# Second layer: the mixed rows of eight tiles turned by VectorE and DRAM in place of TensorE, the last SoLU rows too, and the decay table by four transposes

## The chip, the cores and the metric

One Trainium2 chip (trn2), one of its cores. The metric is the time of one execution on the device in microseconds, the median of three runs. Five engines work side by side, each through its own instructions in order: TensorE (PE in the rows; PEld is its weight load), VectorE (DVE), ScalarE (ACT), GpSimd (POOL) and SyncE (SP). SP computes nothing here; it issues most of the DMAs, in order, and waits in that order too.

## The reference

Three stages, each feeding the next: a retention layer, a top-2 mixture of eight experts, and a dense layer with SoLU and a row norm.

```python
# 1: batch 2, heads 8, seq 768, head_dim 64
state = gamma * state + k_t (outer) v_t;  y_t = scale * q_t @ state
# 2: x is 1536 x 512; w1 512 x 1024, w2 1024 x 512 for each of 8 experts
out[mask] += top2_w[mask, k, None] * (np.maximum(x[mask] @ w1[e], 0.0) @ w2[e])
# 3: w_in 512 x 1024, w_out 1024 x 512
h = x @ w_in
e = np.exp(h - np.max(h, axis=-1, keepdims=True))
solu = h * e / (np.sum(e, axis=-1, keepdims=True) + 1e-09)
ln = (solu - mean) / np.sqrt(var + 1e-06) * g_ln
return ln @ w_out
```

## The kernel before

The 1536 rows are 12 tiles of 128, numbered 0 to 11. The order of work is written out by hand, and each engine gets its instructions in that order. Products are made in two parts: an operand x becomes `hi` (x rounded to the narrower format fp32r, on ScalarE) and `lo` = x - hi (on VectorE), and a product is hi*hi + hi*lo + lo*hi, three passes.

**The start.** `scores(0)` multiplies keys and queries of tile 0 on TensorE, VectorE masks the result (`pm`). `dec_t(0)` (L291) makes a table of decays, one row per column of a head: eight products of a broadcast column of `dec` with the identity, copied to SBUF by ScalarE. `kv(0)` and `y_out(0)` follow on TensorE. They are the first of the retention layer's products; the expert layer comes next, and needs all of them.

**The second layer** (the reference's third stage) is the loop at L1226. Tile i passes through these steps, and iteration i works on several tiles at once:

- `gather` (L815): GpSimd fetches its rows from the experts' results, two gathers of 128 rows.
- `mix(i+4)` (L826): ScalarE and VectorE weigh and add them: 128 tokens x 512.
- `x2_t(i+3)` (L836): TensorE turns them with four transposes into a bank of PSUM; ScalarE copies `x2h` (L850) and VectorE subtracts `x2l` (L851).
- `h_in(i+2, 0)` and `h_in(i+2, 1)` (L854): the product with w_in, 12 passes of 512 columns each, into PSUM bank `d`. `x2_t(i+3)` stands between the two.
- `solu_max(i+2)` and `solu(i+2)` (L901, L906): maximum of the rows (VectorE, L871), exponential (ScalarE, L879), product and norm (VectorE, L880 to L885), which gives `z`.
- `z_turn(i+2)` (L932): VectorE turns `z` in blocks of 32x32 into `zs` (L935), SP writes it to DRAM in four DMAs (`zd`, L938) and loads it back turned (`zc`, L940). That load waits until the four writes have landed.
- `z_parts(i)` (L943): `zh` on ScalarE, `zl` on VectorE.
- `out_mm(i)` (L954): 24 passes with w_out, and in the next iteration `store_out` (L963).

Tiles 0 and 11 do not use `z_turn`: `z_t` (L911) turns them with eight transposes of TensorE. `z_t(11)` stands between `out_mm(9)` and `out_mm(10)`. `out_mm(11)` is made in two column halves, each with a store of its own.

Of the kernel before, what the change touches and what calls it, by code (L numbers as in the profile page):

```python
# [8 lines left out]
F32 = mybir.dt.float32  # L9
F32R = mybir.dt.float32r  # L10
# [5 lines left out]
AF = mybir.ActivationFunctionType  # L16
# [28 lines left out]
def retnet_moe_solu(ctx, tc, qT, kT, k, v, w_gate, w_noise, noise, w1, w2, w_in, w_out, g_ln,  # L45
                    decay, out, dbg=None):
    nc = tc.nc
    B, NC, _, H, D = v.shape
    HP = H // 2
    S = NC * 128  # L50
    NT = B * NC
    E = w1.shape[0]
    DM = H * D
    KD = DM // 128
    FF = w1.shape[2]
    KF = FF // 128
# [7 lines left out]
    dram = ctx.enter_context(tc.tile_pool(name="dram", bufs=1, space=DRAM))  # L64
# [84 lines left out]
    raw_t, unit_t, turn_of = {}, {}, {}  # L149
# [78 lines left out]
    wk = att.enter_context(tc.tile_pool(name="wk", bufs=2))  # L228
# [22 lines left out]
    dec = const.tile([128, 2, NC, H], F32, name="dec")  # L251
# [27 lines left out]
    ident = unit[0][:, G2:G2 + 128]  # L279
# [11 lines left out]
    def dec_t(c):  # L291
        if c >= NC:
            return
        decT[c] = wk.tile([128, HP, 128], F32, tag="decT" if c else "decT0", name="decT", bufs=2 if c else 1)
        if c:
            for hp in range(HP):
                nc.scalar.activation(decT[c][:, hp], decT[0][:, hp], AF.Copy, scale=step[:, c, hp:hp + 1])
            return
        p = bank("c3", (128, HP, 128))
        for h in range(H):  # L300
            r = slice(h % 2 * 64, h % 2 * 64 + 64)
            nc.tensor.matmul(p[r, h // 2, :], dec[:, 1, c, h:h + 1].to_broadcast([128, D]), ident, start=True, stop=True,
                             skip_group_check=True)
        nc.scalar.activation(decT[c], p, AF.Copy)

    def dec_steps():
# [35 lines left out]
    part = const.tile([128, 3], F32, name="part")  # L342
# [54 lines left out]
    for b in range(B):  # L397
        for r in range(2):
            t = wk.tile([128, HP, 128], F32, name=f"S{b}{r}", bufs=1)
# [411 lines left out]
    Y, X2, X2T, PH, ST, Z, RS, ZT = {}, {}, {}, {}, {}, {}, {}, {}  # L811
# [14 lines left out]
    def mix(i):  # L826
        if i >= NT:
            return
        y0, y1 = Y.pop(i)
        t = fr.tile([128, DM], F32, tag="t", name="t")  # L830
        w = top_w[:, i] if i else pick[:, 0]
        nc.scalar.activation(t, y0, AF.Copy, scale=w[:, 0:1])
        nc.vector.scalar_tensor_tensor(t, y1, w[:, 1:2], t, op0=OP.mult, op1=OP.add)
        X2[i] = t

    def x2_t(i):  # L836
        if i >= NT:
            return
        t = X2.pop(i)
        p = bank("a")  # L840
        y = None if i else last_y.pop()
        for d in range(KD):
            c = slice(d * 128, (d + 1) * 128)
            nc.tensor.transpose(p[:, c], t[:, c], ident)  # L844
            if y:
                nc.tensor.matmul(p[:, c], y[:, c], spread.rearrange("p a i -> p (a i)"), start=False, stop=True,
                                 skip_group_check=True)
        hi = fr.tile([128, KD * 128], F32R, tag="x2h", name="x2h")
        lo = fr.tile([128, KD * 128], F32R, tag="x2l", name="x2l")
        nc.scalar.activation(hi, p, AF.Copy)  # L850
        nc.vector.tensor_sub(lo, p, hi)  # L851
        X2T[i] = (hi, lo)

    def h_in(i, s):  # L854
        if i >= NT:
            return
        if s == 0:
            PH[i] = bank(f"d{i % 2}", (128, 2, 512))
        hi, lo = X2T[i]
        n = 0  # L860
        for d in range(KD):
            c = slice(d * 128, (d + 1) * 128)
            f = slice(s * 512, s * 512 + 512)
            wh, wl = unit_t[8 * E + d]
            for x, w in ((hi, wh), (hi, wl), (lo, wh)):
                nc.tensor.matmul(PH[i][:, s, :], x[:, c], w[:, 0, f], start=(n == 0), stop=(n == 3 * KD - 1))  # L866
                n += 1

    def row_max(pool, ph):
        t = pool.tile([128, 16], F32, tag="st", name="st", bufs=3)  # L870
        nc.vector.reduce_max(t[:, 0:1], ph, axis=AX.X)  # L871
        nc.vector.tensor_scalar_mul(t[:, 0:1], t[:, 0:1], -1.0)
        return t
# [27 lines left out]
    def solu_max(i):  # L901
        if i >= NT:
            return
        ST[i] = row_max(m2, PH[i].rearrange("p a f -> p (a f)"))

    def solu(i):  # L906
        if i >= NT:
            return
        Z[i], RS[i] = solu_rows(m2, PH.pop(i).rearrange("p a f -> p (a f)"), ST.pop(i))

    def z_t(i, between=lambda: None):  # L911
        hi = m2.tile([128, KF * 128], F32R, tag="zh", name="zh")
        lo = m2.tile([128, KF * 128], F32R, tag="zl", name="zl")
        z = Z.pop(i)
        ps = []
        for s in range(2):
            p = bank("a")
            for d in range(4):
                f = 4 * s + d
                nc.tensor.transpose(p[:, d * 128:(d + 1) * 128], z[:, f * 128:(f + 1) * 128], ident)  # L920
            c = slice(s * 512, s * 512 + 512)
            nc.scalar.activation(hi[:, c], p, AF.Copy)
            ps.append((p, c))
        for p, c in ps:
# [7 lines left out]
    def z_turn(i):  # L932

        t = m2.tile([128, 4, 256], F32, tag="zs", name="zs")
        nc.vector.transpose(t.rearrange("p g c -> p (g c)"), Z.pop(i).rearrange("p (k g c) -> p g k c", g=4, c=32))  # L935
        d = dram.tile([4, 32, 4, 256], F32, tag="zd", name="zd", bufs=3)
        for a in range(4):
            nc.sync.dma_start(d[:, :, a].rearrange("g i c -> i g c"), t[32 * a:32 * a + 32])  # L938
        t = m2.tile([128, 4, KF, 32], F32, tag="zc", name="zc")
        nc.sync.dma_start(t, d.rearrange("g i a (k j) -> (g i) a k j", j=32))  # L940
        ZD[i] = t

    def z_parts(i):  # L943
        hi = m2.tile([128, KF, 4, 32], F32R, tag="zh", name="zh")
        lo = m2.tile([128, KF, 4, 32], F32R, tag="zl", name="zl")
        t = ZD.pop(i).rearrange("p a k j -> p k a j")
        for k in (slice(0, KF // 2), slice(KF // 2, KF)) if i == 1 else (slice(0, KF),):
            nc.scalar.activation(hi[:, k], t[:, k], AF.Copy)
        ZT[i] = tuple(x.rearrange("p k a j -> p (k a j)") for x in (hi, lo))
        return lambda: nc.vector.tensor_sub(lo, t, hi)  # L950

    OUT = {}

    def out_mm(i, c=slice(0, DM)):  # L954
        hi, lo = ZT[i]
        p = bank("b")[:, c]
        terms = [(z, f, n) for z, ns in ((hi, (0, 1)), (lo, (0,))) for f in range(KF) for n in ns]
        for m, (z, f, n) in enumerate(terms):
            nc.tensor.matmul(p, z[:, f * 128:(f + 1) * 128], unit_t[8 * E + 4 + f // 2][n][:, f % 2, c],  # L959
                             start=(m == 0), stop=(m == len(terms) - 1))  # L960
        OUT[i] = p

    def store_out(i, c=slice(0, DM)):  # L963
        o = m2.tile([128, DM], F32, tag="o", name="o", bufs=3)
        nc.scalar.activation(o[:, c], OUT.pop(i), AF.Copy, scale=RS[i])
        (nc.scalar if c.stop == DM and c.start else nc.sync).dma_start(out[row0(i):row0(i) + 128, c], o[:, c])


    ep = ex_ctx.enter_context(tc.tile_pool(name="ep", bufs=1, reuse_waits="tile"))
# [253 lines left out]
    feed(n_units, n_units)  # L1223
    h_in(1, 1)

    for i in range(NT):  # L1226
        gather(i + 5)
        low = None
        if i == 0:
            z_t(0, lambda: solu_max(1))  # L1230
            solu(1)
            z_turn(1)
            RS[0] = RS[0]()
        else:
            if i < NT - 1:
                low = z_parts(i)
            store_out(i - 1)
        if i + 1 < NT:
            RS[i + 1] = RS[i + 1]()
        h_in(i + 2, 0)  # L1240
        if low:
            low()
        x2_t(i + 3)
        mix(i + 4)
        h_in(i + 2, 1)
        solu_max(i + 2)
        solu(i + 2)
        if i + 2 < NT - 1:
            z_turn(i + 2)
        if i == NT - 2:  # L1250
            z_t(i + 1)
        if i < NT - 1:
            out_mm(i)
        else:
            for c in (slice(0, DM // 2), slice(DM // 2, DM)):
                out_mm(i, c)
                store_out(i, c)
# [135 lines left out]
```

## Time and profile before

| | |
|---|---|
| median of 3 runs | 514.53 us (514.43 to 514.70) |
| the profiled execution | 515.7 us, of which the span from the first to the last instruction is 513.9 us |
| mean granted clock of TensorE | 0.998 |
| busy: TensorE, VectorE, ScalarE, GpSimd | 506.6, 364.6, 233.2, 106.3 us |
| second layer | from 369.1 us (first product of `h_in`) to 510.0 us |

The profile's times are microseconds from the first instruction, of one execution; its span is compared with other spans, its own time with the runs. A busy time counts an instruction from its start to its end, and TensorE's instructions overlap, so the distance from start to start says more than the length of one.

### The profile page before, as it was taken

The numbers are of one execution on the slowest core, as the hardware profiler recorded it, in microseconds if no ns is written. First come the engines' busy times: TensorE is split into PE (matmuls) and PEld (weight loads), VectorE is DVE, ScalarE is ACT, GpSimd is POOL, SyncE is SP. The second block draws the span as 40 slices with busy tenths as digits, with TensorE's granted clock in tenths as the row PEclk, the third lists the DMA queues.
The fourth block names the chain that finished last, engine by engine and source line by source line (L and its number), as shares of the span: only waits on it lengthen the run. The fifth ranks groups of instructions, "written<-read, shape, count | busy, mean of one in ns | idle before, by whom it ended". The sixth has DMA issues, their size and how long they took to land.

```text
span 513.9 us, 8633 instructions
## 1 busy us (share of the span) xinstructions
PE 506.6 (99%) x3068; PEld 463.9 (90%) x3068; DVE 364.6 (71%) x731; ACT 233.2 (45%) x440; POOL 106.3 (21%) x209
## 2 busy tenths in 40 slices
PE   9999999999999999999999999999999999999996
PEld 8898898989999999999999999998878888888885
DVE  4668778756876886877778778799277767666650
ACT  2578734443353443344435443545354644444431
POOL 4124100513002104004003000002244336311120
PEclk9999999999999999999999999999999999999999
DMA  8989531797978988979899968568553565643341
GB/s 259 347 319 368 208 103 42 243 348 266 328 225 230 294 248 203 352 199 283 296 239 324 288 200 237 198 172 222 160 190 106 166 184 149 206 134 103 102 123 47
DMA packets 71857, 111.92 MB, mean 218 GB/s; under 512 B 9760, under 2 KB 37152, under 8 KB 71808
## 3 DMA queue, kind: packets, MB, share of 16 engines
q1 hardware_dynamic: 65952, 96.54, 61.5%
q0 software_dynamic: 4368, 14.29, 8.9%
q10 hardware_dynamic: 1488, 0.48, 0.4%
q8 instruction: 26, 0.43, 0.4%
q14 instruction: 23, 0.19, 0.1%
HBM read 83.50 MB, written 27.79 MB: 217 GB/s over the span
## 4 chain that ended last, share of the span: by engine, by line
PE 90%; issue 5%; DMA 2%; DVE 2%; POOL 1%; ACT 0%; POOLq 0%; ACTq 0%; DVEq 0%
PE c L1077 23%; PE b L959 13%; PE b L729 12%; PE a L729 12%; PE d L866 11%; PE c L1200 3%; PE xr L480 3%; PE s L430 3%; PE c L447 2%; PE c L458 2%; PE c L443 2%; DMA xr<-xd,rows_r 2%; PE a L844 1%; PE c L269 1%; DVE wl L197 0%
## 5 line engine op out<-in xcount | busy, mean ns | idle before, releaser
L201 DVE TENSOR_TENSOR wl<-wr,wh 128x1024 fp32r<-128x1024 f32 x64 | 76.7, 1219 | 13.5 <-ACT wh L200 13.5
L1077 PE MATMUL c<-hh,wh 128*128 128x448 f32 (+5 forms) x224 | 79.1, 353 | 0.0
L1077 PE MATMUL c<-hl,wh 128*128 128x448 f32 (+5 forms) x224 | 78.9, 352 | 0.0
L1077 PE MATMUL c<-hh,wl 128*128 128x448 f32 (+5 forms) x224 | 78.8, 352 | 0.0
L200 ACT ACTIVATE wh<-wr 128x1024 fp32r<-128x1024 f32 x68 | 69.4, 1049 | 8.5 <-DMA wr<-in_moe_w_dram 8.5
L729 PE MATMUL b<-xh,wh 128*128 128x192 f32 (+8 forms) x144 | 47.2, 335 | 0.2 <-ACT xh L644 0.2
L729 PE MATMUL b<-xh,wl 128*128 128x192 f32 (+8 forms) x144 | 46.7, 332 | 0.0
L1077 PEld LDWEIGHTS c<-hh,wl 128*128 128x128 f32 x224 | 42.2, 188 | 1.3
L1077 PEld LDWEIGHTS c<-hh,wh 128*128 128x128 f32 x224 | 42.1, 188 | 1.3
L1077 PEld LDWEIGHTS c<-hl,wh 128*128 128x128 f32 x224 | 42.1, 188 | 1.3
L729 PE MATMUL a<-xh,wh 128*128 128x256 f32 (+7 forms) x128 | 43.1, 341 | 0.0
L729 PE MATMUL a<-xh,wl 128*128 128x256 f32 (+7 forms) x128 | 42.9, 339 | 0.0
L866 PE MATMUL d<-wh,x2h 128*128 128x512 f32 x96 | 38.8, 404 | 0.0
L959 PE MATMUL b<-wh,zh 128*128 128x512 f32 (+1 forms) x104 | 38.4, 375 | 0.0
L959 PE MATMUL b<-wl,zh 128*128 128x512 f32 (+1 forms) x104 | 38.4, 375 | 0.0
L866 PE MATMUL d<-wl,x2h 128*128 128x512 f32 x96 | 37.9, 395 | 0.0
L866 PE MATMUL d<-wh,x2l 128*128 128x512 f32 x96 | 37.8, 394 | 0.0
L1115 POOL COPY pace<-hh 1x1 f32<-1x1 f32 x20 | 9.7, 485 | 135.4 <-ACT hh L733 135.4
L733 ACT ACTIVATE hh<-b 128x192 fp32r<-128x192 f32 (+8 forms) x36 | 17.1, 475 | 43.6 <-PE b L729 40.9
L733 ACT ACTIVATE hh<-a 128x256 fp32r<-128x256 f32 (+7 forms) x32 | 15.9, 496 | 45.8 <-PE a L729 45.8
L1040 ACT ACTIVATE xh<-xt 128x428 fp32r<-128x428 f32 (+5 forms) x24 | 13.0, 540 | 45.1 <-DVE xt L1038 45.1
L1004 POOL DMA_INDIRECT xr<-xd,rows_r x27 | 28.1, 1040 | 25.4 <-DVE rows_r L677 15.9
(258 smaller groups left out, 1091.5 us busy)
## 6 DMA issues: line engine op xcount, KB each, us to landing
wr<-in_moe_w_dram SPq DMA_DIRECT2D x64, 512.0 KB
zd<-zs SPq DMA_DIRECT2D x40, 128.0 KB
zc<-zd SPq DMA_DIRECT2D x10, 512.0 KB
xs<-xr SPq DMA_DIRECT2D x18, 256.0 KB
raw<-in_moe_w_in_dram SPq DMA_DIRECT2D x8, 512.0 KB
raw<-in_moe_w_out_dram SPq DMA_DIRECT2D x8, 512.0 KB
xq<-xs SPq DMA_DIRECT2D x16, 208.0 KB
yg<-yr SPq DMA_DIRECT2D x16, 208.0 KB
```

What stands on the lines that cost most here:

```text
L200: nc.scalar.activation(hi, t, AF.Copy)
L201: (nc.gpsimd if u < LEAD else nc.vector).tensor_sub(lo, t, hi)
L430: nc.tensor.matmul(p[:, s, hp, :], KT[i][r, hp, :], QT[i][r, hp, :], start=True, stop=True)
L480: nc.tensor.matmul(t[:, d // 2, at:at + 128 + G2], XT[i][:, d, :], unit[d // 2][:, G2 - G2 * (d % 2):][:, :128 + G2], start=(d % 2 == 0), ...
L729: nc.tensor.matmul(p, w[:, 0, f * 128:(f + 1) * 128], x[:, d, c], start=(n == 0), stop=(n == len(terms) - 1))
L733: nc.scalar.activation(hh[:, f, c], p, AF.Relu)
L866: nc.tensor.matmul(PH[i][:, s, :], x[:, c], w[:, 0, f], start=(n == 0), stop=(n == 3 * KD - 1))
L959: nc.tensor.matmul(p, z[:, f * 128:(f + 1) * 128], unit_t[8 * E + 4 + f // 2][n][:, f % 2, c], start=(m == 0), stop=(m == len(terms) - 1))
L1004: nc.gpsimd.indirect_dma_start(out=t[b], out_offset=None, in_=xd[:], in_offset=bass.IndirectOffsetOnAxis(ap=rows_r[:, e - 1, b:b + 1], axi ...
L1040: nc.scalar.activation(hi, t, AF.Copy)
L1077: nc.tensor.matmul(py[d][:, :CAPS[e]], c, h[:, f, :CAPS[e]], start=(f == 0 and n == 0), stop=(f == KF - 1 and n == 2))
L1200: nc.tensor.matmul(py, h[:, f, c], w[:, f % 2], start=(f == 0 and n == 0), stop=(f == KF - 1 and n == 2))
```

## The change

Four things are changed.

1. `dec_t(0)`: VectorE writes a broadcast copy `wide` of the decays (128 x 512), and four transposes of TensorE take the place of the eight products.
2. Tiles 4 to 11: `x2_t` is called in iteration 0 only (for tile 3). `x2_turn(i+4)` follows `mix(i+4)`: VectorE turns the mixed rows in 32x32 blocks and SP writes them to DRAM in four DMAs. `x2_load(i+4)` loads them back; it is called inside `z_turn(i+2)`, between z's four writes and z's load. `x2_parts(i+3)` makes `hi` and `lo` from SBUF, between `solu_max(i+2)` and `solu(i+2)`.
3. Tile 11 uses `z_turn` and `z_parts` (the latter with `hi` in two halves), not `z_t`. `out_mm(8)` is split: 12 of its 24 passes stay in place in iteration 8, the other 12 come behind `h_in(11)` in iteration 9, and `store_out(8)` after them.
4. The store of the last column half is scaled half by VectorE, half by ScalarE.

The small tile `st` has four buffers, not three.

```diff
@@ dec_t
+        wide = wk.tile([128, HP, 128], F32, tag="xT", name="wide", bufs=3)
+        nc.vector.tensor_copy(wide.rearrange("p q (s d) -> p (q s) d", s=2),
+                              dec[:, 1, c, :, None].to_broadcast([128, H, D]))
         p = bank("c3", (128, HP, 128))
-        for h in range(H):
-            r = slice(h % 2 * 64, h % 2 * 64 + 64)
-            nc.tensor.matmul(p[r, h // 2, :], dec[:, 1, c, h:h + 1].to_broadcast([128, D]), ident, start=True, stop=True,
-                             skip_group_check=True)
+        for hp in range(HP):
+            nc.tensor.transpose(p[:, hp, :], wide[:, hp, :], ident)
         nc.scalar.activation(decT[c], p, AF.Copy)
...
+    def x2_turn(i):
+        if i >= NT:
+            return
+        t = m2.tile([128, 4, 128], F32, tag="xs", name="xs")
+        nc.vector.transpose(t.rearrange("p g c -> p (g c)"), X2.pop(i).rearrange("p (k g c) -> p g k c", g=4, c=32))
+        d = XD[i] = dram.tile([4, 32, 4, 128], F32, tag="xe", name="xe", bufs=2)
+        for a in range(4):
+            nc.sync.dma_start(d[:, :, a].rearrange("g i c -> i g c"), t[32 * a:32 * a + 32])
+
+    def x2_load(i):
+        if i not in XD:
+            return
+        t = XC[i] = m2.tile([128, 4, KD, 32], F32, tag="xc", name="xc")
+        nc.sync.dma_start(t, XD.pop(i).rearrange("g i a (k j) -> (g i) a k j", j=32))
+
+    def x2_parts(i):
+        if i not in XC:
+            return
+        t = XC.pop(i).rearrange("p a k j -> p k a j")
+        X2T[i] = hi, lo = [fr.tile([128, KD * 128], F32R, tag=n, name=n) for n in ("x2h", "x2l")]
+        hi, lo = (x.rearrange("p (k a j) -> p k a j", k=KD, j=32) for x in (hi, lo))
+        nc.scalar.activation(hi, t, AF.Copy)
+        nc.vector.tensor_sub(lo, t, hi)
...
@@ z_turn
             nc.sync.dma_start(d[:, :, a].rearrange("g i c -> i g c"), t[32 * a:32 * a + 32])
+        x2_load(i + 2)
         t = m2.tile([128, 4, KF, 32], F32, tag="zc", name="zc")
@@ z_parts
-        for k in (slice(0, KF // 2), slice(KF // 2, KF)) if i == 1 else (slice(0, KF),):
+        for k in (slice(0, KF // 2), slice(KF // 2, KF)) if i in (1, NT - 1) else (slice(0, KF),):
...
@@ store_out
+        if c.start and c.stop == DM:
+            m = (c.start + c.stop) // 2
+            nc.vector.tensor_scalar_mul(o[:, m:c.stop], p[:, m - c.start:], RS[i])
+            nc.scalar.activation(o[:, c.start:m], p[:, :m - c.start], AF.Copy, scale=RS[i])
+            nc.scalar.dma_start(out[row0(i):row0(i) + 128, c], o[:, c])
...
@@ the loop
+    HALF = 12
     for i in range(NT):
...
-            if i < NT - 1:
-                low = z_parts(i)
-            store_out(i - 1)
+            low = z_parts(i)
+            if i != NT - 3:
+                store_out(i - 1)
...
         if low:
             low()
-        x2_t(i + 3)
+        if not i:
+            x2_t(i + 3)
         mix(i + 4)
+        x2_turn(i + 4)
         h_in(i + 2, 1)
+        if i == NT - 3:
+            out_mm(i - 1, part=slice(HALF, 3 * KF))
         solu_max(i + 2)
+        x2_parts(i + 3)
         solu(i + 2)
-        if i + 2 < NT - 1:
+        if i == NT - 3:
+            store_out(i - 1)
+        if i + 2 < NT:
             z_turn(i + 2)
-        if i == NT - 2:
-            z_t(i + 1)
-        if i < NT - 1:
+        if i == NT - 4:
+            out_mm(i, part=slice(0, HALF))
+        elif i < NT - 1:
             out_mm(i)
```

Three places in the engines' orders. TensorE at the start, before: the scores of tile 0 (`s`), the table's products (from `dec`), `kv(0)` (from `vp` and `kn`), `y_out(0)` (from `pm` and `vp`).

```order
L430 MATMUL s<-qt,kt 128x128 x8
L302 MATMUL c_285<-unit_169,dec 64x128 x8
L458 MATMUL c_256<-vp,kn 128x128 x4
L447 MATMUL c_313<-pm,vp 64x128 x8
L430 MATMUL s<-qt,kt 128x128 x8
```

The same place now:

```order
L431 MATMUL s<-qt,kt 128x128 x8
L304 MATMUL c_287<-unit_169,wide 128x128 x4
L459 MATMUL c_256<-vp,kn 128x128 x4
L448 MATMUL c_311<-pm,vp 64x128 x8
L431 MATMUL s<-qt,kt 128x128 x8
```

The transposes stand where the products stood, and need `wide`; on VectorE the copy that writes `wide` (L300) stands behind both masks `pm` (L435).

SP in one iteration of the second layer, before: z's four writes, z's load, the store of an earlier tile.

```order
L938 DMA zd<-zs 32x4x256 x4
L940 DMA zc<-zd 128x1024
L966 DMA out_dram<-o 128x512
L938 DMA zd<-zs 32x4x256 x4
L940 DMA zc<-zd 128x1024
```

And now, with x2's four writes (`xe`) and its load (`xc`):

```order
L864 DMA xe<-xs 32x4x128 x4
L965 DMA zd<-zs 32x4x256 x4
L870 DMA xc<-xe 128x512
L968 DMA zc<-zd 128x1024
L1001 DMA out_dram<-o 128x512
L864 DMA xe<-xs 32x4x128 x4
```

x2's writes stand ahead of z's, x2's load behind z's writes.

ScalarE in one iteration, before: `zh`, the store's scaling, the squares of z, `x2h` of tile i+3, the weighing of `mix`, the exponential of tile i+2 (from `d`).

```order
L948 ACTIVATE zh<-zc 128x1024
L965 ACTIVATE o<-b,st 128x512
L890 ACTIVATE ee,st<-z 128x1024
L850 ACTIVATE x2h<-a 128x512
L832 ACTIVATE t<-y_4780,top_w 128x512
L879 ACTIVATE ee,st<-d_4897,st 128x1024
```

And now:

```order
L976 ACTIVATE zh<-zc 128x1024
L1000 ACTIVATE o<-b,st 128x512
L917 ACTIVATE ee,st<-z 128x1024
L833 ACTIVATE t<-y_4795,top_w 128x512
L878 ACTIVATE x2h<-xc 128x512
L906 ACTIVATE ee,st<-d_4916,st 128x1024
```

`x2h` of tile i+3 now reads the loaded tile `xc`, and stands directly ahead of the exponential of tile i+2.

## Rows read from the trace of the kernel before

**Rows 1.** The page's busy times: us, share of the span, instructions of each engine.

```profile
PE 506.6 (99%) x3068; PEld 463.9 (90%) x3068; DVE 364.6 (71%) x731; ACT 233.2 (45%) x440; POOL 106.3 (21%) x209
```

**Rows 2.** TensorE's waits: us in total, times, longest us; three of five.

```profile
PE c L269 <- DVE ones L266: 1.1, 1, 1.1
PE a L1034 <- DMA xr<-xd,rows_r: 0.8, 1, 0.8
...
PE a L844 <- DVE zl L925: 0.2, 1, 0.2
```

**Rows 3.** The chain that ended last, its end: start us, us, what.

```profile
477.46 0.44 PE a L844 x4
...
480.69 5.50 PE b L959 x24
486.19 5.58 PE d L866 x24
...
497.27 1.06 PE a L920 x8
...
509.56 0.47 ACT o L965
```

**Rows 4.** Timeline of the start, TensorE and VectorE: start us, us, instruction.

```profile
4.79 1.88 PE L430 MATMUL s<-qt,kt 64*128 64x128 f32 x16
6.61 1.09 PE L302 MATMUL c<-unit,dec 128*64 128x128 f32 x16
7.63 1.16 PE L458 MATMUL c<-vp,kn 128*128 128x128 f32 x8
...
9.74 1.16 PE L430 MATMUL s<-qt,kt 64*128 64x128 f32 x16
...
6.73 1.29 DVE L434 TENSOR_TENSOR pm<-s,causal 128x512 f32<-128x512 f32 x2 [0.55 <-PE s L430]
```

**Rows 5.** Single tiles' instructions: duration ns min/median/max, first and last start us.

```profile
L885 DVE TENSOR_SCALAR z<-ee,st x12: 811/812/816, 379.8 to 496.4; 128x1024 f32<-128x1024 f32 x12
L935 DVE STREAM_TRANSPOSE zs<-z x10: 1245/1245/1246, 390.3 to 486.1; 128x1024 f32<-128x1024 f32 x10
L850 ACT ACTIVATE x2h<-a x12: 579/598/602, 367.9 to 477.9; 128x512 fp32r<-128x512 f32 x12
L851 DVE TENSOR_TENSOR x2l<-a,x2h x12: 679/691/693, 368.5 to 478.6; 128x512 fp32r<-128x512 f32 x12
...
L821 POOL DMA_INDIRECT y<-yg,slot_y x22: 940/947/1336, 363.5 to 445.7; - x22
...
DMA to landing us min/median/max: 3.5/3.7/5.4
```

**Rows 6.** Timeline of tile 10's SoLU and turn: VectorE, ScalarE and SP (SPq).

```profile
480.79 1.23 DVE L871 TENSOR_REDUCE st<-d 128x1 f32<-128x1024 f32 x1 [1.53 <-PE d L866]
...
482.32 1.11 ACT L879 ACTIVATE ee<-d,st 128x1024 f32<-128x1024 f32 x1 [3.79 <-DVE st L872]
...
487.41 1.77 SPq L938 DMA_DIRECT2D zd<-zs  x4
491.11 0.34 SPq L940 DMA_DIRECT2D zc<-zd  x1
...
495.09 1.07 ACT L948 ACTIVATE zh<-zc 128x1024 fp32r<-128x1024 f32 x1 [0.49 <-DMA zc<-zd]
```

**Rows 7.** Timeline of the loop's first iterations, tiles 2 to 4.

```profile
393.20 1.22 DVE L871 TENSOR_REDUCE st<-d 128x1 f32<-128x1024 f32 x1
...
399.81 1.75 SPq L938 DMA_DIRECT2D zd<-zs  x4
...
405.44 0.39 PE L866 MATMUL d<-wh,x2h 128*128 128x512 f32 x1
...
415.19 0.34 SPq L940 DMA_DIRECT2D zc<-zd  x1
...
420.55 1.06 ACT L948 ACTIVATE zh<-zc 128x1024 fp32r<-128x1024 f32 x1 [5.45 <-DMA zc<-zd]
```

More of the change, by code (lines that the diff above doesn't have):

```diff
@@ L852, in x2_t @@
         X2T[i] = (hi, lo)
+    XD, XC = {}, {}
+    def x2_turn(i):
[19 more added lines that the diff above has]
+        nc.vector.tensor_sub(lo, t, hi)
     def h_in(i, s):
@@ L869, in row_max @@
     def row_max(pool, ph):
-        t = pool.tile([128, 16], F32, tag="st", name="st", bufs=3)
+        t = pool.tile([128, 16], F32, tag="st", name="st", bufs=4)
         nc.vector.reduce_max(t[:, 0:1], ph, axis=AX.X)
@@ L952, in retnet_moe_solu, with out_mm @@
     OUT = {}
-    def out_mm(i, c=slice(0, DM)):
+    def out_mm(i, c=slice(0, DM), part=slice(0, 3 * KF)):
         hi, lo = ZT[i]
-        p = bank("b")[:, c]
+        if not part.start:
+            OUT[i] = bank("b")[:, c]
         terms = [(z, f, n) for z, ns in ((hi, (0, 1)), (lo, (0,))) for f in range(KF) for n in ns]
-        for m, (z, f, n) in enumerate(terms):
-            nc.tensor.matmul(p, z[:, f * 128:(f + 1) * 128], unit_t[8 * E + 4 + f // 2][n][:, f % 2, c],
+        for m, (z, f, n) in list(enumerate(terms))[part]:
+            nc.tensor.matmul(OUT[i], z[:, f * 128:(f + 1) * 128], unit_t[8 * E + 4 + f // 2][n][:, f % 2, c],
                              start=(m == 0), stop=(m == len(terms) - 1))
-        OUT[i] = p
     def store_out(i, c=slice(0, DM)):
         o = m2.tile([128, DM], F32, tag="o", name="o", bufs=3)
-        nc.scalar.activation(o[:, c], OUT.pop(i), AF.Copy, scale=RS[i])
-        (nc.scalar if c.stop == DM and c.start else nc.sync).dma_start(out[row0(i):row0(i) + 128, c], o[:, c])
+        p = OUT.pop(i)
+        if c.start and c.stop == DM:
[3 more added lines that the diff above has]
+            nc.scalar.dma_start(out[row0(i):row0(i) + 128, c], o[:, c])
+        else:
+            nc.scalar.activation(o[:, c], p, AF.Copy, scale=RS[i])
+            nc.sync.dma_start(out[row0(i):row0(i) + 128, c], o[:, c])
     ep = ex_ctx.enter_context(tc.tile_pool(name="ep", bufs=1, reuse_waits="tile"))
```

## The prediction

> **What bounds the kernel now.** I read the page's busy times first: TensorE is busy for 506.6 us of 513.9 [rows 1]. The list of what TensorE waited for says the same from the other side: five waits, 2.6 us in all, the longest of them 1.1 us before its first product and 0.8 us for a gather in the first expert layer; one of 0.2 us lies in the second layer [rows 2]. The chain that ended last shows what TensorE does there: per tile two halves of `h_in` (5.58 together), between them the four transposes of `x2_t` (0.44), then `out_mm` (5.50), with no gap [rows 3]. So a TensorE instruction that is taken out gives back its whole time, and anything TensorE has to wait for that it did not wait for before is added in full. The question is what the new waits cost.
>
> **A. The transposes of eight tiles go.** `x2_t` of tiles 4 to 11 took 0.44 us each [rows 3]: 8 x 0.44 = -3.5.
>
> **B. The transposes of tile 11's SoLU rows go.** `z_t(11)` took 1.06 us on TensorE [rows 3]: -1.1.
>
> **C. The decay table.** Before, its eight products ran at 6.61, right behind the first scores, while VectorE multiplied those by the mask from 6.73 to 8.02; `kv(0)` followed at 7.63 [rows 4]. Now VectorE first writes `wide`, and that copy stands behind both mask products. It is not in this trace. From above it costs no more than one mask product (1.29 / 2 = 0.65), from below no less than a quarter of that row's pair, 0.3; the nearest row is `z`, also one source and one result in SBUF, 0.81 for 1024 columns [rows 5], so some 0.5 for 512. TensorE can thus start its four transposes (0.44) at about 8.6, and `kv(0)` at 9.0: 1.4 us late (1.2 to 1.6). Nothing takes this up: behind `kv(0)` stand all other products in TensorE's order, and its one longer wait further on, the 0.8 us for a gather [rows 2], moves along, since the gather's list comes out of those products. +1.4, for an edit that shortens TensorE's own work by half a microsecond.
> The Trainium skill ("VectorE: DVE Perf Modes", section "Mode 2×_2P — use both read ports for one tensor") says that a one-source fp32 operation from SBUF to SBUF yields two results a cycle; at the 0.96 GHz of its specifications 512 columns would then be 0.27 us by estimate, and the delay 1.2. No run here shows that copy yet.
>
> **D. The first tile that comes by DRAM.** Tile 4 is the first. Its row of the maximum of tile 2 started at 393.20 and the first z write of tile 2 was issued at 399.81, 6.61 later [rows 7]. VectorE now also transposes tile 4 ahead of that maximum (half of the 1.25 for 1024 columns [rows 5], 0.62), so z writes start at 400.4 and, with 1.75 of issuing, SP comes to `x2_load(4)` at 402.2: it stands behind those four. How long that load takes from issue until ScalarE may read is the number that decides most. It is not in the trace. From below: 2.4, what the last z write (128 KB) needed (the fourth of four issues of 1.77 together begins by 488.7, SP released at 491.1 [rows 6]). From above: 4.0, what the 512 KB load of z needs (491.11 to 495.09 [rows 6]). A gather of the same 256 KB in the same rows of 2 KB took 3.5 at best, with 0.94 of issuing instead of 0.34 [rows 5], so 2.9; and the load goes out behind z writes in flight. I take 3.2. Landing is then at 405.4, `hi` is done 0.60 later on ScalarE, `lo` 0.69 after that on VectorE [rows 5], 406.7. `h_in(4)` began at 405.44 [rows 7] and is now due 0.44 earlier, 405.0; its third product is the first to need `lo`, 0.46 in. It starts at 406.3: +1.3 (0.5 with a load of 2.4, 2.1 with 4.0).
>
> **E. The tiles after it.** In ScalarE's queue the `hi` of tile i+3 now stands ahead of the exponential of tile i+2. So there is a circle: exponential, z, z writes, load, `hi`, next exponential. In tile 10 it takes 6.86 from the exponential (482.32) to the end of the z writes' issue (489.18) [rows 6], then the load, then some 0.55 for `hi` until the next instruction: 7.41 + 3.2 = 10.6. TensorE needs 5.58 + 5.50 = 11.08 for a tile [rows 3]. So the circle is shorter by 0.45, and after tile 4's wait the load gets 0.45 earlier against TensorE with each tile: no further wait, 0. By tile 11 that is seven times 0.45, 3.2 us, and it must be: with half of `out_mm(8)` (2.75) moved behind `h_in(11)`, that product starts 2.75 earlier against its input. It holds while the load takes up to some 3.3 us.
> VectorE and ScalarE have room for the rest: `lo` and the transposes (0.69 and 0.62) take the place of the `x2l` that went and fall into VectorE's wait for the exponential.
>
> **F. The last tile.** From tile 10's maximum (480.79, 0.1 behind its last product [rows 3]) to ScalarE reading its turned z (495.09) it was 14.3 [rows 6]. The first half of `hi` is half of zh's 1.07, so some 0.6 with its start: 14.9, and 0.1 from the last product to the maximum: 15.0. TensorE's work between `h_in(11)` and `out_mm(11)` is 2.75 + 5.50 + 5.50 = 13.75. So +1.3 (0.9 to 2.0), a little more than B saved. Without the moved half it would be 4.
>
> **G. The end.** The last rows' 0.47 on ScalarE [rows 3] become two halves on two engines: -0.2 (0 to 0.25).
>
> **Sum:** -3.5 - 1.1 + 1.4 + 1.3 + 0 + 1.3 - 0.2 = -0.8. The profiled execution took 515.7 (span 513.9 and 1.8 around it), the median of the runs is 514.53; a difference carries over, so I predict **513.7**.
>
> **The rivals.**
> 1. *The circle is the bound.* If the load takes over 3.67 us, 7.41 and the load are more than 11.08, and every tile waits. With 4.0: tile 4 waits 0.8 longer than in D, tiles 5 to 10 wait 0.33 each (2.0), tile 11 waits 0.33 and the 2.75 that the moved half no longer covers, 3.1: +5.9 on the sum, about 519.6; with 3.75 some 517.5. For it: in an early tile, where gathers run beside it, the load of z took from 415.19 to 420.55, 5.4 instead of 4.0 [rows 7], and x2's own writes now add 256 KB a tile to the queues. Against: z's load has twice the bytes. This is the case that ends slower.
> The Trainium skill ("DMA: Bandwidth & Descriptors", section "Queues, rings and completion order") says that a DMA's semaphore counts up only after every earlier write of that DMA engine, of any queue; by it the load would not be released before the z writes ahead of it have landed, and gathers beside it would hold it up. The trace agrees as far as it goes: the slow load of 5.4 us is one with a gather beside it.
> 2. *Only tile 11 is late.* With a load of 3.3 to 3.67 us the circle is shorter than TensorE's tile, but the lead by tile 11 is less than 2.75: at 3.5 it is 1.2, so `h_in(11)` waits 1.5, and with 0.3 in D the sum is +1.0: 515.5.
> 3. *The covers are better than I think.* A load of 2.4 leaves 0.5 in D, the copy costs 1.2, the last wait is 0.9: -3.5 - 1.1 + 1.2 + 0.5 + 0.9 - 0.2 = -2.2: 512.3. If no wait shows at all, it is -4.8: 509.7; the order of the start alone speaks against that.
> 4. *TensorE is slow again after the wait in C.* The first scores took 1.88 us, the next 1.16 [rows 4]: TensorE got faster while it worked. If the idle 2 us undid that, the 2 us of products behind it would take 1.6 times as long: +1.3, 515.0. The granted clock was 0.998 over this span, so it did not fall again here; but this run had no such gap.
>
> **How the numbers follow.** Chances: the forecast 0.40, rival 1 0.18, rival 2 0.18, rival 3 0.17, rival 4 0.07. A measurement of this kernel can tell some 0.2%, 1.0 us, from no change. The forecast with its own bounds (load 2.6 to 3.3, copy, last wait) reaches from 512.8 to 514.3, about half of it below 513.5; rival 3 is faster; rival 2 is about half within and half above; rivals 1 and 4 are mostly slower. Faster 0.38, same 0.30, slower 0.32. Range: 511.8 leaves out the best of rival 3, 518.0 the worse half of rival 1.
>
> **What the profile after would show.** C: TensorE waiting for VectorE's `wide` near 6.6 us for some 2 us, `kv(0)` at 9.0. A: `h_in` of tiles 4 to 11 as one piece of 5.58. D: one wait of TensorE at `h_in(4)` for VectorE's `x2l` or ScalarE's `x2h`. E: from tile 5 on a period of 11.08; were the circle the bound, a wait at each `h_in`. F: `out_mm(11)` waiting about 1.3 for ScalarE's `zh`. The prediction is wrong if ScalarE waits for `xc` much longer or shorter than 3.2 us after its issue.

## The result and the profile after

The changed kernel took **517.34 us** (median of 6 executions, 517.03 to 518.6), the kernel before, on the same chip, 514.62 (514.43 to 515.0). The ratio is 1.0054, 95% interval 1.0041 to 1.0068: 2.7 us slower where 0.8 faster was forecast. The profiled execution of the changed kernel took 517.06 (span 515.2).

The page's busy times: TensorE works 4.2 us less than in [rows 1]. A, B and the half microsecond of the table's products make 5.1; where the other 0.9 went was not traced.

```profile
PE 502.4 (98%) x3016; PEld 459.2 (89%) x3016; DVE 371.8 (72%) x741; ACT 232.8 (45%) x440; POOL 111.8 (22%) x209
```

What TensorE waited for (total, times, longest in us), to be held against [rows 2]:

```profile
PE c L304 <- DVE wide L300: 1.8, 1, 1.8
PE b L988 <- ACT zh L976: 1.8, 2, 1.6
PE c L269 <- DVE ones L266: 1.1, 1, 1.1
PE a L1069 <- DMA xr<-xd,rows_r: 0.8, 1, 0.8
PE d L893 <- ACT x2h L878: 0.6, 1, 0.6
PE a L641 <- DMA xr<-xd,rows: 0.5, 1, 0.5
```

Three come from the change: the table's copy, the turned z (`zh`) and the x2 by DRAM (`x2h`). The last line, another gather, isn't on the list of [rows 2], but it is on that of a second execution of the kernel before (0.5). The list leaves out the restart and the slower first products behind a wait, so the losses below are read from where the same product starts in both traces.

The start, TensorE and VectorE of the changed kernel, against [rows 4]:

```profile
5.02 1.90 PE L431 MATMUL s<-qt,kt 64*128 64x128 f32 x16 [0.15 <-DMA kt<-in_kT_dram]
8.74 0.63 PE L304 MATMUL c<-unit,wide 128*128 128x128 f32 x4 [1.83 <-DVE wide L300]
9.21 1.06 PE L459 MATMUL c<-vp,kn 128*128 128x128 f32 x8
...
6.97 1.29 DVE L435 TENSOR_TENSOR pm<-s,causal 128x512 f32<-128x512 f32 x2 [0.41 <-PE s L431]
8.17 0.42 DVE L300 COPY wide<-dec 128x512 f32<-128x512 f32 x1
```

The copy stands behind both masks, as C had it, and `kv(0)` starts at 9.21 instead of 7.63: +1.6, of which 0.2 is a later `kt`. The copy itself took 0.42, inside the prediction's 0.3 to 0.65. By the rate alone that the Trainium skill gives ("VectorE: DVE Perf Modes", section "Mode 2×_2P — use both read ports for one tensor"), its 512 columns would be 0.27 by estimate; the row has 0.15 beside that, and the row decides.

Tile 4's way through DRAM, SP and ScalarE, and the turn of tile 11 (against [rows 6, 7]):

```profile
402.10 1.75 SPq L965 DMA_DIRECT2D zd<-zs  x4
404.01 0.34 SPq L870 DMA_DIRECT2D xc<-xe  x1
405.86 0.34 SPq L968 DMA_DIRECT2D zc<-zd  x1
...
407.07 0.63 ACT L878 ACTIVATE x2h<-xc 128x512 fp32r<-128x512 f32 x1 [2.98 <-DMA xc<-xe]
407.60 1.10 ACT L906 ACTIVATE ee<-d,st 128x1024 f32<-128x1024 f32 x1
...
476.02 2.99 SPq L965 DMA_DIRECT2D zd<-zs  x4
...
488.90 1.23 DVE L898 TENSOR_REDUCE st<-d 128x1 f32<-128x1024 f32 x1 [0.22 <-PE d L893]
...
495.51 1.77 SPq L965 DMA_DIRECT2D zd<-zs  x4
499.32 0.34 SPq L968 DMA_DIRECT2D zc<-zd  x1
...
503.36 1.15 ACT L976 ACTIVATE zh<-zc 128x512 fp32r<-128x512 f32 x2 [4.56 <-DMA zc<-zd]
```

x2's load took 407.07 - 404.01 = 3.06 us until ScalarE could read; to the landing it was 2.7 to 3.1 over the eight tiles. That was the number called decisive, and the value taken (3.2) held. `h_in` of tiles 4 to 11 starts at 407.75, 419.19, 430.24, 441.29, 452.33, 463.38, 474.43 and 482.75: from tile 5 to 10 a period of 11.05 without a wait, where it was 11.51 before. The start of `hi` gets further ahead of its `h_in` with each of these tiles, from 1.6 us at tile 5 to 4.0 at tile 10; at tile 11 it is 0.8.

The last rows, VectorE and ScalarE, against the one scaling in [rows 3]:

```profile
510.16 0.35 DVE L996 TENSOR_SCALAR o<-b,st 128x128 f32<-128x128 f32 x1 [4.39 <-PE b L988]
510.60 0.37 ACT L997 ACTIVATE o<-b,st 128x128 f32<-128x128 f32 x1 [2.76 <-DVE o L996]
510.99 0.37 ACTq L998 DMA_DIRECT2D out_dram<-o  x1
```

The halves don't run side by side: ScalarE's is released by VectorE's. From the first scaling to the store's issue it is 0.83 us; with one scaling of 0.47 it is 0.5.

### The profile page after: what moved, and what is told of

It is laid out like the page before. It is cut to its first block, busy times and chain, and to the rows that moved or that the text cites. A ratio compares the mean times of both kernels' runs of the same rounds, so it can differ in the third digit from the quotient of the medians.

```text
span 515.2 us, 8630 instructions
## 1 busy us (share of the span) xinstructions
PE 502.4 (98%) x3016; PEld 459.2 (89%) x3016; DVE 371.8 (72%) x741; ACT 232.8 (45%) x440; POOL 111.8 (22%) x209
## 4 chain that ended last, share of the span: by engine, by line
PE 68%; DMA 13%; DVE 6%; issue 6%; SPq 3%; ACT 2%; POOL 1%; ACTq 0%; POOLq 0%; DVEq 0%
PE c L1112 23%; PE a L730 12%; PE b L730 12%; DMA xe<-xs 4%; PE c L1235 3%; DMA zd<-zs 3%; PE xr L481 3%; PE d L893 3%; PE s L431 3%; SPq L965 3%; PE c L448 2%; PE b L988 2%; DVE zs L962 2%; PE c L459 2%; PE c L444 2%
```

## The experiments

Medians, and ratios to the kernel before from runs on the same chip; "us" is (ratio - 1) x 514.5. The edits are given shortened, with words in place of some lines.

| kernel | median | ratio (95%) | us |
|---|---|---|---|
| changed kernel | 517.34 | 1.0054 (1.0041 to 1.0068) | +2.8 |
| a1_before_again | 514.53 | 1.0009 (0.9998 to 1.0019) | +0.5 |
| a2_old_table | 513.94 | 1.0005 (0.9989 to 1.0020) | +0.3 |
| a3_old_store | 516.11 | 1.0042 (1.0027 to 1.0056) | +2.2 |
| a4_x2_alone | 512.78 | 0.9965 (0.9952 to 0.9978) | -1.8 |
| b1_load_first | 526.17 | 1.0223 (1.0198 to 1.0249) | +11.5 |
| b2_copy_ahead | 515.65 | 1.0015 (1.0005 to 1.0025) | +0.8 |
| b3_table_alone | 516.87 | 1.0049 (1.0036 to 1.0062) | +2.5 |
| b4_last_alone | 517.96 | 1.0065 (1.0046 to 1.0083) | +3.3 |
| c1_rest | 522.07 | 1.0150 (1.0128 to 1.0172) | +7.7 |
| c2_whole | 522.62 | 1.0163 (1.0141 to 1.0185) | +8.4 |
| c3_te_last | 518.43 | 1.0079 (1.0050 to 1.0107) | +4.1 |
| d2_whole_only | 519.31 | 1.0085 (1.0054 to 1.0115) | +4.4 |
| e1_one_earlier | 512.99 | 0.9963 (0.9945 to 0.9981) | -1.9 |
| e2_last_whole | 513.90 | 0.9991 (0.9972 to 1.0009) | -0.5 |
| e3_table_scalar | 512.67 | 0.9970 (0.9959 to 0.9982) | -1.5 |
| f1_parts_first | 512.83 | 0.9968 (0.9956 to 0.9980) | -1.6 |
| f2_load_behind | 512.81 | 0.9965 (0.9953 to 0.9978) | -1.8 |
| f3_copy_scalar | 515.02 | 1.0012 (1.0002 to 1.0021) | +0.6 |

The theory: the loss is a sum of small waits that stand against what TensorE gives back. The rivals: x2's transfers slow the second layer as a whole, or something lies outside the spans.

### The kernel before once more

> The kernel before, unchanged, to see how far its time and its profiled span move between executions, since the two profiles stand 1.3 us apart and the two medians 2.7. If the loss is the sum of small waits that the profile of after shows, the profile of before shown here is one of its longer executions, the median is 514.6 again, and a second profile has a span of 512.8 to 513.2. If something outside the spans were behind the difference (the start or the landing of the last store), the second span is 513.9 again while the time stays at 514.6.

The median is the same and the second profile has a span of 512.2, so the profile from which the prediction was worked out was a long execution; what lies outside the span was 1.75 to 1.90 in all 11 executions. Where the 1.7 us went shows at two places of the two traces. Start of the second one:

```profile
4.76 1.16 PE L430 MATMUL s<-qt,kt 64*128 64x128 f32 x16
5.85 1.09 PE L302 MATMUL c<-unit,dec 128*64 128x128 f32 x16
6.88 1.16 PE L458 MATMUL c<-vp,kn 128*128 128x128 f32 x8
```

The first scores took 1.16 here and 1.88 in [rows 4], so `kv(0)` starts at 6.88, not 7.63. The same microsecond of both traces, before first, then this run (start:end, us, PE busy (products), granted clock, DMA share, GB/s):

```profile
5.00:6.00 1.00, 1.00 (x10) 1.00 1.15 318
5.00:6.00 1.00, 1.00 (x18) 1.00 1.15 335
```

The views print a granted clock of 1.00 for both, but in each trace the record of that clock begins only with its first stretch at 2.4 GHz, and where there is no record they print 1.00. It begins at 6.34 in the trace of [rows 4] and at 4.57 here. The scores start in pairs, and in every trace the pairs follow each other every 0.21 us ahead of the record's start and every 0.11 behind it: TensorE was still at 1.2 GHz for most of the first scores there, and at 2.4 for all of them here.

The 0.8 us for a gather in the first expert layer [rows 2] are not there at all. The rest of TensorE's starts keeps its distance within 0.35 between the two traces. And 0.5 is what the same kernel can differ from itself by these ratios.

### The table

b3 is the kernel before with the new table alone, a2 the changed kernel with the old one. b2 moves the copy on VectorE, f3 gives it to ScalarE:

```diff
 # b2: between scale_v(0) and scores(0)
+nc.vector.tensor_copy(wide, dec broadcast)     # moved here from dec_t
 # f3
-nc.vector.tensor_copy(wide, dec broadcast)
+nc.scalar.activation(wide, dec broadcast, AF.Copy)
```

> The changed kernel with the decay table made by the eight products of before. If the loss is the sum of small waits: kv(0) starts at 7.6 instead of 9.2, no wait for wide, and the time falls by 1.4 to 1.6 against the changed kernel, to about 515.8. If x2's transfers slow the second layer as a whole, the same fall, since the two don't touch. If TensorE takes up a late start further on, no fall: 517.3.

> The kernel before with the new decay table and nothing else. If the wait for wide is added in full: +1.4, 516.0. If TensorE takes up the late start further on: 514.6.

> The changed kernel with VectorE's copy into wide put ahead of both mask products of tile 0, right behind the scaling of v. If the copy's place in VectorE's order is the whole cost of the table, the four transposes run right behind the first scores at about 6.6, kv(0) starts at 7.2 to 7.5 instead of 9.2, and the kernel is 1.7 to 2.0 faster: about 515.4. If the copy delays the mask products and those the products behind them, kv(0) starts no earlier than 7.9 and about 1.2 is gained. If the transposes themselves are slow, it is 517.3.

> The changed kernel with the copy into wide made by ScalarE, which is idle there, and nothing else. If the table's whole cost is the copy's place behind both masks on VectorE, kv(0) starts at 6.8 to 7.2 and the kernel gains 2.2 to 2.5, as much as with the old table: 515.0. If half of the table's cost is something else (the transposes, TensorE's clock), the gain is 1.2: 516.1.

The table costs 2.5 us by both a2 and b3, more than the 1.4 to 1.6 expected. Its place is nearly all of it: with the copy ahead of the masks 2.0 come back, with ScalarE 2.2. The start with ScalarE's copy:

```profile
4.92 1.28 PE L431 MATMUL s<-qt,kt 64*128 64x128 f32 x16
6.45 0.66 PE L304 MATMUL c<-unit,wide 128*128 128x128 f32 x4 [0.25 <-ACT wide L300]
6.94 1.06 PE L459 MATMUL c<-vp,kn 128*128 128x128 f32 x8
...
5.76 0.63 ACT L300 ACTIVATE wide<-dec 128x512 f32<-128x512 f32 x1 [1.56 <-DMA dec<-in_decay_dram]
```

The 2.5 are made of two things, and now and then of a third. First, `kv(0)` is late. In the seven traces with the eight products it starts at 6.88 to 7.63, depending on when TensorE's clock rose, on the mean at 7.15; in the five with the copy behind both masks it starts at 8.72 to 9.21, on the mean at 9.05. That is 1.9, where the one profile of [rows 4] gives 1.6. Then the wait for the gather in the first expert layer: 0.2 to 1.0 in all 13 profiles with the four transposes, the early starts of f3 (0.8) and f1 (0.6) too, and in six of the seven with the products it is not on the list of waits (0.8 in that of [rows 2]). It goes with the table's form and not with the start; what makes it so is open. The third is TensorE's clock, which fell in b1 during the wait for `wide`, and in none of the other four traces with that wait. Stretches of b1 (columns as above):

```profile
5.00:6.00 1.00, 1.00 (x16) 1.00 1.10 325
7.00:8.00 1.00, 0.00 (x0) 0.69 1.14 354
9.00:10.00 1.00, 1.00 (x6) 0.50 1.06 391
12.00:14.00 2.00, 2.00 (x20) 0.50 0.98 101
14.00:16.00 2.00, 2.00 (x18) 0.95 0.94 317
```

TensorE was at 2.4 GHz, waited 1.97 for `wide`, and ran at 1.2 until some 14 us. From `kv(0)` to the retention layer's last product it took 63.1 us, in the changed kernel 60.7. This is rival 4, in one execution; the profile of the changed kernel shows 1.00 behind its wait of 1.8.

### The store

```diff
-nc.vector.tensor_scalar_mul(second half) ; nc.scalar.activation(first half)
+nc.scalar.activation(both, scale=RS[i])
```

> The changed kernel with the last rows scaled by ScalarE alone, as before. If the two halves run one behind the other because they read one bank or write one tile, the time from the first scaling to the issue of the store falls from 0.83 to 0.5, and the kernel is 0.3 to 0.7 faster: 516.6 to 517.0. If the halves had been worth what I took (0.2), it is 0.2 slower: 517.5.

2.2 instead of 2.8: the halves cost 0.6 by the medians where I took a gain of 0.2, but the two intervals overlap, so the runs alone don't show it. The traces show 0.3: the issue comes 0.5 behind the scaling's start again (510.00, then 510.50), not 0.83. Whether the halves are in sequence for their common bank or their common tile was not tried apart.

### x2 alone

a4 has x2's way through DRAM for tiles 4 to 11 and nothing else of the change.

```diff
+x2_turn(i + 4) ; x2_load in z_turn ; x2_parts(i + 3)
 # dec_t, z_t(11), out_mm(8), store_out as before
```

> The kernel before with the one edit that the mixed rows of tiles 4 to 11 go by VectorE and DRAM; the table, tile 11's SoLU rows and the last store are those of before, and out_mm(8) isn't split. If the loss is the sum of small waits, this part alone pays: -3.5 of transposes, +1.2 at h_in(4), +0.3 to 0.5 for the turned z of tile 1, so -1.8, about 512.8, without a wait at h_in(11). If the transfers of x2 slow the second layer as a whole, it gives nothing: 514.6 with waits in many tiles.

-1.8, as the sum of waits has it; the rival of the slow second layer falls. No wait at `h_in(11)`. This part of the change is the one that pays, and no later kernel beats it by more than the intervals.

### The last tile alone

b4 is the kernel before with `z_turn(11)`, its `hi` in halves and `out_mm(8)` split.

```diff
+z_turn(11), z_parts(11) in two halves
+out_mm(8) terms 0..11 before, 12..23 behind h_in(11)
-z_t(11)
```

> The kernel before with tile 11's SoLU rows by DRAM, its hi in two halves and out_mm(8) split around h_in(11); table, store and the transposes of x2 stay. If the loss is a sum of small waits: -1.06 of transposes on TensorE and a wait of 1.5 to 1.9 at out_mm(11): +0.5 to +0.9, 515.3. If the last tile's rows were late only because of x2's transfers in the queues, the wait is 1.0 or less and the time 514.5 or less.

Missed: +3.3. `out_mm(11)` waits 3.0 by the list, and TensorE's clock falls in that wait, which cost some 1.3 more behind it (stretches as above):

```profile
502.00:504.00 2.00, 0.00 (x0) 0.93 0.68 266
504.00:506.00 2.00, 1.95 (x9) 0.50 0.02 7
506.00:508.00 2.00, 2.00 (x14) 0.72 0.35 128
```

From the last z write's issue to z's load 3.3 us passed (499.16 - 495.88), in the changed kernel 2.0. In that time a packet of 16 KB of the queue that loads instructions took 1.34 us. The two go together in all the traces: from the first of z's writes to the issue of the load that waits for their landing it is 4.2 to 5.6 us (median 5.0) in the 30 cases with such a packet in between, and 3.8 on the median in the 174 without one, two of which are above 4.8. Another 0.6 lies outside the span (2.2 to 2.5 in all six executions, against 1.7 to 1.9 elsewhere); open.

### x2's load ahead of z's writes

```diff
 # z_turn
+x2_load(i + 2)
 for a in range(4): nc.sync.dma_start(...)     # z's writes
-x2_load(i + 2)
```

> The changed kernel with the load of x2 issued ahead of z's four writes on SyncE instead of behind them. If the loss is a sum of small waits: ScalarE has the rows of tile 4 some 1.8 us earlier, the waits of h_in(4) (1.15) and of h_in(11) (0.3) go, z's writes start 0.3 later, which lies under the load's lead except at out_mm(11), +0.3 there: about -1.1, 516.2. If the x2 traffic itself slows the layer, its order changes nothing: 517.3.

Missed on both sides: 8.7 slower than the changed kernel. SP of this kernel over one tile:

```profile
441.25 0.34 SPq L870 DMA_DIRECT2D xc<-xe  x1
441.63 1.87 SPq L966 DMA_DIRECT2D zd<-zs  x4
446.17 0.34 SPq L968 DMA_DIRECT2D zc<-zd  x1
446.55 0.43 SPq L1001 DMA_DIRECT2D out_dram<-o  x1
447.03 2.79 SPq L864 DMA_DIRECT2D xe<-xs  x4
453.95 0.34 SPq L870 DMA_DIRECT2D xc<-xe  x1
454.33 1.86 SPq L966 DMA_DIRECT2D zd<-zs  x4
```

x2's writes are out by 449.82, and the load that reads them is issued at 453.95, 4.1 later. VectorE had turned z by 450.42 (its instruction: 449.17, 1.25 long), but z's writes stand behind the load. Now SP stands twice a tile for a landing, 4.1 for x2's writes and 2.7 for z's: one round takes 454.33 - 441.63 = 12.7 against TensorE's 11.05, and six `out_mm` wait for `zh`. In the changed kernel's order the first landing is over while SP waits for z anyway.

Three more kernels have this order, all with the copy ahead and the old store too:

```diff
 # c1: copy ahead, old store, load first
 # c2: c1, and out_mm(8) whole behind h_in(11)
 # c3: c1, and z_t(11), out_mm(8) as before
```

> The changed kernel with three things put otherwise: the copy into wide ahead of the mask products, the load of x2 ahead of z's writes, and the last rows scaled by ScalarE alone. If the waits add up, it is the sum of the three: -1.8, -1.1 and -0.4, about 514.0, below the kernel before. If x2's traffic slows the layer, only the table and the store are gained: 515.1.

> As the kernel with three things put otherwise, and the whole of out_mm(8) behind h_in(11), not its second half. If the wait at out_mm(11) is only cover that is missing (13.75 against some 15.6), 2.75 more of cover takes it away: -1.9, about 512.1, unless h_in(11), which comes 2.75 earlier against its x2, waits; with the load ahead of the writes it has the lead for it, so up to 0.5. If the queues are the bound, the wait only moves to h_in(11): 514.0.

> As the kernel with three things put otherwise, but tile 11's SoLU rows are turned by TensorE as before, with out_mm(8) in one piece. If the waits add up: +1.06 for the transposes and -1.9 for the wait at out_mm(11), about 513.2. If the last tile by DRAM costs no more than it saves, 514.0 or more.

All three are slow by the load's order, and say little else; c3 is 3.6 faster than c1, so the last tile by DRAM is dear here too. c2 computes tile 8's product and rows twice, by a slip in the edit (3064 products, not 3016), so it is no evidence on `out_mm(11)`.

e1 takes the wait away from the load: x2 is mixed, turned and written one tile earlier (tile 4 stays on TensorE), so what the load reads has long landed.

```diff
-gather(i + 5) ; mix(i + 4) ; x2_turn(i + 4)
+gather(i + 6) ; mix(i + 5) ; x2_turn(i + 5)   # and gather(5), mix(4) ahead
 # z_turn: x2_load(i + 2) ahead of z's writes, as in b1 ; the rest as before the change
```

> The kernel before with the mixed rows of tiles 5 to 11 by DRAM, mixed, turned and written one tile earlier than in the changed kernel; tile 4 keeps TensorE's transposes. x2's load stands ahead of z's four writes, as in the kernel with the load first, but now the writes that it reads have landed long before. If the loss of the kernel with the load first came from SyncE standing at the load until x2's own writes had landed, this kernel loses nothing by that order, no h_in waits, and seven tiles give 7 x 0.47 = 3.3 less about 0.3 for zh(1): 511.5 where before has 514.5. If it came from the transfers themselves (the load ahead of z's writes in the queues), it is slow like that kernel, above 520. If the wait of h_in(4) belongs to the first tile by DRAM whatever its lead, h_in(5) waits 1.1: 512.6.

-1.9, 1.5 short of what was expected, but with the same order of issue none of b1's loss. So that was SP standing at the load. No `h_in` waits either: the wait in D is lateness of x2's chain. But a new one shows once, 1.9 at an `out_mm` whose z load took 6.5 instead of 4.0 (415.24 to 421.73), and the executions spread from 509.97 to 514.62.

### Cover at the last tile

d2 is the changed kernel with the whole of `out_mm(8)` behind `h_in(11)`.

```diff
-out_mm(8) terms 0..11 ; h_in(11) ; out_mm(8) terms 12..23
+h_in(11) ; out_mm(8)
```

> The changed kernel with the whole of out_mm(8) behind h_in(11) instead of its second half, and nothing else. If h_in(11) and out_mm(11) each wait for a chain of fixed length (x2's from the exponential before, z's from the maximum), what is moved out of one cover is missing in the other: h_in(11), 2.75 earlier against its rows, waits some 3.1 instead of 0.4, out_mm(11), with 16.5 of cover instead of 13.75, waits 0 instead of 1.6 to 1.9, together +0.9 against the changed kernel, 518.2. If x2's chain had room at tile 11, only the wait at out_mm(11) goes: -1.7, 515.6.

The waits are those of the first theory: 3.2 for x2 (longest 2.7), none at `out_mm(11)` (the 0.3 is `out_mm(1)`). From TensorE's list:

```profile
PE d L893 <- ACT x2h L878: 3.2, 2, 2.7
...
PE b L988 <- ACT zh L976: 0.3, 1, 0.3
```

The stretches behind the long wait:

```profile
484.00:486.00 2.00, 2.00 (x7) 0.63 0.67 258
486.00:488.00 2.00, 2.00 (x6) 0.52 0.00 0
488.00:490.00 2.00, 2.00 (x11) 1.00 0.58 124
```

The time is 1.6 over the changed kernel's, where 0.9 was expected; the executions spread from 516.36 to 521.88, so the medians don't tell the two apart. In this execution TensorE ran at 1.2 GHz for some three microseconds behind the wait of 2.7: its products started every 0.43 us instead of every 0.23, which lost 1.6. Cover only moved from one wait to the other.

e2 is e1 with the last tile by DRAM and `out_mm(8)` whole behind `h_in(11)`; e3 adds the table with ScalarE's copy.

```diff
 # e2: e1 +
+z_turn(11), out_mm(8) behind h_in(11)
-z_t(11)
 # e3: e2 + wide by ScalarE, four transposes
```

> As the kernel with x2 one tile earlier, and tile 11's SoLU rows by DRAM with the whole of out_mm(8) behind h_in(11). If cover is all that the last tile lacks (16.5 against some 15.7), neither h_in(11) nor out_mm(11) waits and 1.06 more is gained: 510.4. If the last tile's turn costs more than its cover in any case, out_mm(11) waits 1 or more and the time is 511.5 or above.

> As the kernel before this one in the list, and the decay table by four transposes with the copy into wide made by ScalarE, which is idle there, instead of VectorE. If the copy's place behind VectorE's masks is the whole cost of the new table, kv(0) starts at 6.8 to 7.2, no later than before: 510.0 to 510.4. If the table costs 2 us in any form, 512.4.

Both miss, by 3.5 and some 2.5 us. e2 has its second value's time (511.5 or above) without its wait at `out_mm(11)`. e3 comes near its second value (512.4), but not for the reason given there: `kv(0)` starts at 7.04, as the first has it. x2 is early now, yet `h_in(11)` loses 1.9 at its third product in both. VectorE in e3:

```profile
476.59 1.23 DVE L898 TENSOR_REDUCE st<-d 128x1 f32<-128x1024 f32 x1 [3.35 <-PE d L893]
...
477.93 0.69 DVE L879 TENSOR_TENSOR x2l<-xc,x2h 128x512 fp32r<-128x512 f32 x1
```

`lo` of tile 11 stands behind the maximum of tile 10, which waits for the last product ahead of `h_in(11)`. e2 also had one wait of 1.6 for `zh` like e1's. f1 puts `hi` and `lo` first:

```diff
-solu_max(i + 2) ; x2_parts(i + 3)
+x2_parts(i + 3) ; solu_max(i + 2)
```

> As the kernel with the table's copy on ScalarE, x2 one tile earlier and out_mm(8) moved whole, with tile i+3's hi and lo written ahead of tile i+2's row of the maximum, so that VectorE makes lo of tile 11 without waiting for the last product of h_in(10). If the 1.9 us at h_in(11) there is VectorE's order alone, it goes and nothing takes its place (out_mm(11) had 16.5 of cover): 512.7 - 1.9 = 510.8. If the last tiles' chain is too long anyway, the wait moves to out_mm(11): 512.7.

The wait left `h_in(11)`, and 1.3 came up at `out_mm(11)`; the time is that of e3. VectorE again sets it:

```profile
477.03 1.23 DVE L898 TENSOR_REDUCE st<-d 128x1 f32<-128x1024 f32 x1 [2.62 <-PE d L893]
...
482.37 1.25 DVE L962 STREAM_TRANSPOSE zs<-z 128x1024 f32<-128x1024 f32 x1
483.54 1.18 DVE L978 TENSOR_TENSOR zl<-zc,zh 128x1024 fp32r<-128x1024 f32 x1
484.64 1.21 DVE L898 TENSOR_REDUCE st<-d 128x1 f32<-128x1024 f32 x1
```

Tile 11's maximum starts 7.6 behind tile 10's, with no idle time ahead of it, since the whole SoLU of tile 10 and a `zl` stand ahead of it on VectorE, while TensorE now needs only 5.6 between the two `h_in`. Two microseconds of the 16.5 of cover are lost there.

```diff
 # f2: f1, with x2_load(i + 3) behind z's load, not ahead of z's writes
```

> As the kernel with hi and lo first, with x2's load behind the load of z of the iteration before instead of ahead of z's writes. If the single waits of 1.7 to 1.9 us at out_mm(3) in two of the kernels with x2 one tile earlier came from x2's writes and load running beside z's, the spread of the times gets smaller and the median 0.5 to 1 lower than the kernel with hi and lo first: 510.0. If the order of x2's load no longer matters once its writes have landed, the two are equal: 510.8.

Equal to f1: with x2 a tile early the load's place no longer matters. The executions of both keep within 1.0, and f1 has the load where e1 has it; so that place alone doesn't make e1's spread, which stays open.

## Why the prediction was wrong

It said -0.8 and +2.7 was measured. By its own steps:

- **A** held: the period of `h_in` fell from 11.51 to 11.05, 8 x 0.46 = -3.7 (predicted -3.5).
- **B** held: -1.1.
- **C** is the step that failed most, in size: 2.5 instead of 1.4. The place of the copy was right. But the sum took `kv(0)` of before at 7.63 from one execution that was 0.75 late itself, since TensorE's clock rose late in it (1.9 late by the means of all traces), and it let the gather's wait "move along", where that wait is 0.2 to 1.0 with the new table and mostly absent with the old.
- **D** held: `h_in(4)` starts 12.30 behind `h_in(3)` (395.45), and `h_in(5)` 11.44 behind `h_in(4)`, where the period is 11.05. Of these 1.6, 0.5 were lost at `out_mm(1)` and 1.2 at `h_in(4)` for `hi` and `lo` (predicted 1.3), with the load at 3.06 (3.2 taken).
- **E** held for tiles 5 to 10, whose period shows no wait and whose lead grows as forecast. For tile 11 the lead fell short by 0.3, since z's four writes ahead of its load took 2.99 to issue instead of 1.75 (476.02 to 479.01), with an instruction packet of 1.35 at 476.8. That isn't the same in every execution: with the same second layer a2 and b2 lose 1.1 there, a3 0.6, and f3, where no such packet falls into the issue of z's writes, nothing. And one wait was missed: the 0.5 at `out_mm(1)` for `zh(1)`, which the 0.44 of tile 4's transposes had covered until A removed them (e1 keeps them, and has no wait there).
- **F** was too small: 1.9 instead of 1.3. The 0.1 from the last product to the maximum held. The transfers took 0.2 more (14.46 from the maximum to ScalarE's read, for 14.3), the half 0.1 more, the cover was 0.1 less (13.63), and the other 0.3 are what the list of waits leaves out: the first product behind a wait doesn't overlap the one before it, and the next comes late. With it B is a loss, and b4 shows that the last tile alone can cost more.
- **G** had the wrong sign: +0.3 in the trace (0.6 by a3's median) instead of -0.2. The two engines ran in sequence.

With these the sum is -3.7 - 1.1 + 2.5 + 0.5 + 1.2 + 0.3 + 1.9 + 0.3 = +1.9, and +2.2 with a3's 0.6, at the lower end of the interval of +2.1 to +3.5. The rest was not traced; the same kernel can differ from itself by 0.5, and the terms but for C are of one execution. Of the rivals, 1 did not come (the load never took 3.67), 2 only in part (0.3), 3 not; 4 was seen in b1, not in the profile of the changed kernel, and b4 and d2 show the same behind other waits. The sign was wrong because C, E, F and G each erred on the same side, not through any one mechanism; that the chain of x2 keeps up with TensorE's tile was right, and a4 gains what A, D and the wait at `out_mm(1)` say (-2.0, measured -1.8).

## What to carry to other kernels

Price a new instruction by what stands ahead of it on its engine when its input is there, and look for an engine that is idle then: the same copy cost 2.5 us behind two masks and 0.3 on ScalarE. Issue a load that reads what its own queue has just written behind everything that needn't wait for those writes, or write a tile earlier; and count moved work as cover once, since what it hides in one wait it bares in another. Work out a small sum from more than one execution of before where its terms lie at a place, such as the start, that differs between executions by as much as the forecast.

## What the runs showed of the hardware that was not expected

- TensorE's granted clock fell to 1.2 GHz during or shortly behind seven waits, of 1.8 (c2, c3), 2.0, 2.1 and 2.6 (b1), 2.7 (d2) and 3.0 us (b4), and stayed there for 3 to 7 us. It stayed at 2.4 through others as long: 1.9 (d2, for `wide`), 2.1 (b1) and 2.4 (c1). The length of the wait alone doesn't decide it. In d2 the fall cost 1.6, more than half of the wait again.
- At the start TensorE runs the same 34 products from 1.05 us on in all 20 traces, and its clock rises anywhere between 3.7 and 6.8 us. The first scores follow that: 1.16 us where the record begins at 4.57 (a1), 1.28 at 5.20 (f3), 1.46 at 5.63 (a3), 1.88 at 6.34 ([rows 4]), 1.90 at 6.60 (the changed kernel) and 2.08 at 6.81 (b3). What sets the moment is open.
- An instruction packet of 16 KB within z's four writes goes with a landing some 1.3 us later (30 cases, at b4 above).
- In b1 x2's four writes of 64 KB took 4.1 us from the last issue until the load that reads them, z's four of 128 KB 2.7: half the bytes, one and a half times the time. Over the first six tiles x2's took 3.7 to 4.4, in the last two 2.7 to 2.9, so their size alone doesn't make it; they stand right behind a load of 512 KB and a store of 256 KB in the queue. What does is open.
